# A conformer block on one core: a new written-out order of the instruction blocks, with new PSUM banks

## The chip, the cores and the metric

The kernel runs on one core of a Trainium2 chip. Each of the core's engines takes its instructions from a queue of its own, in the order in which the program wrote them: TensorE (PE, with its weight loads shown apart as PEld), ScalarE (ACT), VectorE (DVE), GpSimd (POOL) and SyncE (SP, which here only issues DMAs). Engines meet through semaphores. TensorE writes its results to PSUM, which has eight banks; ScalarE and VectorE read them there and write to SBUF.

The metric is the device time of one execution in microseconds, as the median of several runs. Next to it stands one profiled execution, whose trace gives the start and duration of each instruction. Its span runs from the first to the last instruction.

## The reference, cut to what matters

The input x has 2 sequences of 4000 tokens with 144 features. All tensors are bf16.

```python
h = _silu(_layernorm(x) @ w_ff1a) @ w_ff1b;  x = x + 0.5 * h       # 144 -> 576 -> 144
q, k, v = split(_layernorm(x) @ w_qkv)                              # 4 heads of 36
p = softmax(q @ k.T * 36 ** -0.5);  x = x + (p @ v) @ w_o           # 4000 x 4000 a head
a, b = split(_layernorm(x) @ w_pw1);  h = a * sigmoid(b)
x = x + _silu(depthwise_conv5(h)) @ w_pw2
h = _silu(_layernorm(x) @ w_ff2a) @ w_ff2b;  x = x + 0.5 * h
return _layernorm(x)
```

The attention is the bulk: 2 sequences, 4 heads and 4000 x 4000 scores each, 128 million exponentials.

## The kernel before, in words

**Tiling.** The 8000 tokens are 16 chunks of 500, eight to a sequence. A step of the attention takes one chunk of queries against 64 keys, for all four heads. Its scores fill two PSUM banks (128 partitions x 1000 values, as four matmuls of 64 x 500, `scores` and `emit_S`, L1770 and L1783). ScalarE turns them into a PT tile (bf16, 128 x 1000) by one Exp instruction (`emit_exp`, L1797), or VectorE does it with integer arithmetic in five instructions on two PT tiles (`dve_tile`, L1811). TensorE then multiplies the PT tile with the values (`o_quads`, L1847; "PV" below, four matmuls PS<-PT,VA) and accumulates in banks 6 and 7. Banks 0 to 5 are shared by the scores and by all other work, so that at most three pairs of score banks are in flight, and fewer while other work holds some. There are 15 PT tiles.

**The other work** runs beside the attention in small pieces: layer norms (statistics ST on VectorE, the power RS and the normalised rows XN on GpSimd), transposes through DRAM (tensor `rows`: four writing DMAs rows<-XN or rows<-AN and two reading ones XT<-rows, issued by SyncE, `blocks`, L1032), the feed-forward layers (HT; tanh tiles TH on ScalarE), the q, k, v projections, the gated unit and convolution (U, SW), and the residuals (X). GpSimd copies the edge columns between neighbouring chunks (`halo`, L1490, and L1505). Before about 20 us and after about 840 us there is no full attention to hide this work: the first chunk has to be made, and the last chunks have to be finished and stored.

**What sets the order.** A planner in the kernel's code writes all instructions down, in small blocks, with costs of its own. What the engines get is then decided by two tables written out by hand, ORDER (L38) and PLACES (L111). `Rec.reorder` (L281) sorts the blocks of each engine by ORDER: the table has one letter for each block of an engine, and the letter's place in ALPHABET (L37), less 45, says how many places the block moves from where the planner had it (P is no move, Q one later, O one earlier; ~ begins a wider move).

```python
            shift.append(c - 45)
...
        for i, blk in enumerate(blocks):
            at[i + shift[i]] = blk
        lines[e] = [o for blk in at for o in blk]
```

PLACES has a digit for each of 1724 PSUM tiles: the first bank that the tile takes. `reorder` then works out anew which reader of a bank has to be done before the next tile may be written there, and `finish` (L365) turns all dependences into semaphore waits. Nearly all instructions are recorded through one helper, so that the profile shows them under the same line, L419, and they are told apart by their tiles.

Of the kernel before, what the change touches and what calls it, by code (L numbers as in the profile page):

```python
# [39 lines left out]
        "PPPPPPPPQOPPPPROQNPPQRPQLPPRPVPSPNIZMWOMVVL~OVKLJ~OOJJNSNLMMMNPNPKSOOJ[JZKMXNKOG]NJHEKNNNE_MMMadMJLL"  # L40
        "mTLI?LJLEMZPbJNJMGrLLLLkfJKKKKKWKNNVJMKgBJJJ[QddGGMIFKEcQKLJFKNKKNNKPUMOMWTMYVIRLLISKOLPQQRPRPJQUNPQ"
        "OQKPPPPPYOOOOYNNNOMhTNLVXLMIMOSXKILOKN`NNRRNHQOXROMQOTKOUQQQTQUS]PT[`P2ALQXDMKILMNTQLSKNRNUN_PMMNOWN"
        "]NNOOSKPRPDIOQOY__MWNNN]NHMNQCGMQJNWNORTOMRRTLTPNSOBOP^UNNQMMTLNPTLLTMNOWNOOOXNOPLOPNQQMTTNNNNRSO]OQ"
        "OPPGPNROMQQLPPQOPVOcNNNNPMTNNOM]]LNNKMNPWOPNJUOOCOOXOOYZOMKcLLWXJKKSWKHKKVJNNKNORPNPQOQOSOOVNOYZMMMM"
        "NNOMPXPKOOVQMNPVOPHPYMNOQNNPN[]^LMM]MKWKKKLJKLVLP`LN_NLNOMOQNKMRMNLPPPQOS[P[MOPISOKNQMIPRPSPLQNPWORO"
        "QQKLVOQRN[QQQQJFPPPPKQQSPRKQQLPPPQVPPQOPUUOOPNCXORRNYVSSNG[MPUZPPAOKAOMUNNPVOLTUOL]KLNRPMMSNNNNdZNQM"
        "MMNNQMSLLTYMOMSHVKUO]JJ`RKTNQKMFLNQNW[]NLPHLNQNRMNFPPPS]OOLOOPPSLNNNQOSOPN`SNOMNO_PMMNOMOOLPNPYVL^[Q"
        "LNKKFMQM[TLMOOQWNQVQMKYNRNXNO8NRMMNYOOQNN^OOOQOIOSP[OPRPZGOOPN]YMNNNO<VNNKMNOYPNOOOTQM]MVJSMMRMKSPUM"
        "HOPNSOOOSOPNTPNOOROOQVNOPNO^RPQMVOHNQNLPRPJPXOOPNPNOOPXXNNNOOOWNIOOOORUOPKOSNROTXKOW[KOKLN[RZIMOIKNN"
# [12 lines left out]
        "OTKOPSSUHNSOOSHO^PUOOQNNGO_NNSMM[TMKSLMKYMJOMbQNLRLMXMNSMMMMYTMQWHMJPSLLQMVOROOLQUZXOMIMWPKMKMOQNQO`"
        "OPR`LMVLNLNPNJhPSHN]RHQMI^NQIMKTNVIOLHSXIQZIOVJMbMKZSPKQSIYKDLRKLMMSNTfNORUMRGLSULNWZLF_KP^KHYJPLLEM"
        "M]LL]cNUMVPKRLJLGPWPN;NNNZNOUNNZOLLSPMQIRSKPL]^_MMMMMMOMKMMMSSLRNKPPWOVNOOLNNQRNOVTNNWXLLLQMSLSKMOQO"
        "TPNRZ_MKNNNWQLZ^LJHLQKKXLWMKMMPTQVK[QOLUPMZPMMQVMPVVLMYLOMQUN`NNNP[QN%SLMMMOWQMI[QMSMKNNVSMOLLTNQNNP"
        "WQV[LPNJKPSKOOLPQOQO_QNNXNNVMMMOMKMP_OOOOOQNQOPKWOOPKQN`YOOROOPFOQNROEQQUYJVNNPJOOJ[OOPNPROLYTNKMNTM"
        "NNNP^[NOMNNQMMOLNN]PNOOR[OPKQN_ZLNESMOOKHOM[NPPLPNOOPPMQSTMNPQQQQRSQRRTCQVNGRNOMTTTMMNUPPQHNQSPMYVTQ"
        "KLLSSOIJPSSPTMKORNOQOPPPPPPSORNSMRNRRRNQQRPFRPQQQQQQRPFQO"
    ),
    "act": (  # L70
        "PPPPPPPPPPPPPRTNNOOPPQOPPPPPPXPNOSNNNNPPPPPPQRSOLOQZQORKRSLLOQQJPPPPQQNQOPPPPPPPPPQQQMPPPPPPPPPPPPRO"
        "OPQOPQQNPPPPPPPPPPPPPPPPPPPPPPPPPPPPPPPPPPPPPPPPPPPPPPPPPPPPPPPPPPPPPQOPRORNSNOOPPPPPPPPPQOPPPPPPPPP"
        "QOPPPPPPPPPPPQOPPPPPPPPPPPPQOPPPPPPPPPPPRPNPQOPPPPPRPNPPPPPPPPPPPPPPPPPPPPPPPPPPPPPPPPPPPPPPPPPPQOQQ"
        "NPPPPPPPPPPPPPPPPPPPPPPPPPPPPPPPPPPPPPPPPPPPPPPPPPPPPPPPPPPPPPPPPPPPPQOPPPPPPPPPPPPPPQOPPQOPPPPPPPPP"
        "PQOPPPPPPPPPPPPPPPPPPPPPPPPPPPROOPQOPPPPPPPPPPPPPPPPPPPQOPPPPQOPPPPPPPPPPPPPPPPPTOOPQQLPPPPPPPPPPPPP"
        "PPPPPQOPPQOPPPPPPPQOPPPPPPPPPPQOPPQOPPPPPQQQQLQQNPPPPPPQOPPPPPPPPPPPPPPPQOPPPQOPPPPPPPPPPPPPPPPPPPPQ"
        "OPPPPPPPTOPNOROOPPPPPPPPPPPPPPPQOPQOPPPPPPPPPPQOPPPPPPPPPPPQOPPPPPPPPPPPPPPPPQOPPPPPPPPPPQOPPPPPPPPP"
        "PPPRPNPPPPPPPPPQOPPPPPPPPPPPPPPPPPPPPPQRNOPPQQNPPPPPPPQQNPPPPPPPPPPPPPPPPPQOQOPPQOPPPPPPPPPPQOQOPPPP"
        "PPPQOQOPPPPPPPPPPPPPPPPPPPPPPPPPPPPQQNPPPPPPPPPPPPPPPPPPPPQOPPPPPPPPPPPPPPROOPPPPPPPPPPPPPPPPPPPPPQQ"
        "NPPPPQOPPPPPPPQQNPPPPPPPPPQOPPPPPPPPPPPPQOPPPPPPPPPPPPPPPPPPPPPPPPPPPPPPPPPPPPPPPPPPPPPPQOPPPPPPPPPP"  # L80
        "PPPPPPPPPPPPPPPPPPPPPPPPPPPPPPPPPQOSPNRNOQOUQNPMOPPPRORNQNPPPPPPQOROQQMPPPPPPQOPPPWORNNNOO"
    ),
# [23 lines left out]
    "sp": (  # L106
        "PPQOPPPPQOPPPPPPPPPPPPPPPPROOPPPPSOSNNOPPPPPPPPPPPPPPPPPQOPPQOPPQOPPQOQOPPPPPPQOPPPPPTOPNRNOVOOOOOOP"
        "WOVNNNNOMPPSORNQMPPPPSOOOPPWOQNNOOOPPPPQSNOOPPQQN"
    ),
}  # L110
PLACES = (  # L111
    "2354210532250435102310543130213550204405323252304105230054110122532115431241204124012410314032034023"
    "4203420340243310402430043213420342040324303025420342034203420342034203420342034203420342024042045012"
    "4024120552405240424052405240425025203540240532052402405240524052402205304230532052305240524052405245"
# [2032 lines left out]
```

## Time and profile before

| | |
|---|---|
| median of 3 runs | 879.83 us (879.45 to 880.12) |
| the profiled execution's own time | 878.56 us |
| its span | 876.7 us |
| granted TensorE clock, mean | 0.998 |
| TensorE, ScalarE, VectorE, GpSimd busy | 96%, 97%, 94%, 34% of the span |
| DMA | 28.82 MB, 33 GB/s |

The busy time of an engine counts each moment once. ScalarE's records of neighbouring instructions overlap, since the next one starts before the last one's end is recorded; the pace is therefore read as busy time of a group divided by its count, not from the mean duration of one record. An idle stretch is put down to the instruction that ended it.

### The profile page before, as it was taken

Reading aid. Unit: us, or ns where it says so; the run is one execution under the profiler, and the core shown is the slowest. Engines: PE = TensorE matmul, PEld = TensorE weight load, DVE = VectorE, ACT = ScalarE, POOL = GpSimd, SP = SyncE. Lnnn points to the kernel's source line nnn. Section 1 sums busy time; section 2 is a strip of 40 time slices with the busy share of each in tenths; the row PEclk is TensorE's granted clock in tenths of the full one; section 3 lists DMA queues with packets and bytes.
Section 4 is the critical chain, followed back from the end, with each engine's and each line's share of the span. In section 5 each row is a group of like instructions: output and inputs, shape, how many; then the busy total and the mean of one; then the engine's idle time right before and its main releaser. Section 6 shows DMA issues by size and latency. Waiting matters only on the chain.

```text
span 876.7 us, 27043 instructions
## 1 busy us (share of the span) xinstructions
PE 844.4 (96%) x11419; PEld 385.5 (44%) x11419; DVE 825.6 (94%) x1821; ACT 848.4 (97%) x1098; POOL 293.8 (34%) x573
## 2 busy tenths in 40 slices
PE   8999999999999999999999999999999999999996
PEld 6544444334444434443444444444434443344465
DVE  8978999999999999999989999899999999999987
ACT  6799999999999999999999999999999999999985
POOL 6650441341425231152324426222420115013434
PEclk9999999999999999999999999999999999999999
DMA  3221101211121020212001120100210010001111
GB/s 100 52 52 35 26 15 41 58 29 38 37 48 41 16 52 9 45 22 53 16 4 35 28 46 16 36 24 16 49 26 22 16 31 19 21 14 37 29 25 35
DMA packets 114353, 28.82 MB, mean 33 GB/s; under 512 B 101090, under 2 KB 114230, under 8 KB 114230
## 3 DMA queue, kind: packets, MB, share of 16 engines
q1 hardware_dynamic: 112646, 26.39, 13.7%
q8 instruction: 90, 1.47, 0.7%
q10 hardware_dynamic: 1584, 0.69, 0.3%
q14 instruction: 33, 0.27, 0.1%
HBM read 13.44 MB, written 13.61 MB: 31 GB/s over the span
## 4 chain that ended last, share of the span: by engine, by line
PE 39%; ACT 35%; DVE 21%; POOL 3%; issue 1%; DMA 0%; POOLq 0%; DVEq 0%
PE PS L419 39%; ACT PT L419 32%; DVE PT L419 10%; ACT TH L419 3%; DVE ST L419 3%; DVE HT L419 2%; DVE X L419 2%; DVE XN L419 2%; POOL RS L419 1%; POOL XN L419 1%; DVE QT L419 1%; DVE AN L419 0%; DVE KT L419 0%; DMA X<-in_x_dram 0%; DVE VA L419 0%
## 5 line engine op out<-in xcount | busy, mean ns | idle before, releaser
L419 ACT ACTIVATE PT<-PS 128x1000 bf16<-128x1000 f32 (+1 forms) x818 | 751.0, 1048 | 3.7 <-PE PS L419 2.6
L419 PE MATMUL PS<-QT,KT 64*64 64x500 bf16 x3968 | 419.2, 383 | 15.6 <-ACT PT L419 8.5
L419 PE MATMUL PS<-PT,VA 64*37 64x500 bf16 x4728 | 403.1, 372 | 1.0 <-DVE QT L419 0.7
L419 DVE TENSOR_SCALAR PT<-PS 128x500 int16<-128x500 f32 x380 | 251.2, 669 | 6.2 <-PE PS L419 4.7
L419 PEld LDWEIGHTS PS<-QT,KT 64*64 64x64 bf16 x3968 | 125.1, 104 | 231.8 <-ACT PT L419 122.4
L419 POOL TENSOR_SCALAR RS<-ST 125x4 f32<-125x4 f32 x130 | 39.5, 304 | 484.0 <-DVE ST L419 477.7
L419 PEld LDWEIGHTS PS<-PT,VA 64*37 64x37 bf16 x4728 | 141.9, 96 | 91.4 <-issue 13.1
L419 DVE TENSOR_SCALAR PT<-PT 128x1000 uint16<-128x1000 uint16 x380 | 153.1, 418 | 2.1 <-PE PS L419 0.9
L419 POOL TENSOR_SCALAR XN<-X,RS 125x144 bf16<-125x144 bf16 x260 | 146.8, 594 | 8.3
L419 DVE TENSOR_TENSOR PT<-PT 128x1000 bf16<-128x1000 bf16 x190 | 127.9, 675 | 1.1
L419 ACT ACTIVATE TH<-PS 128x500 bf16<-128x500 f32 (+3 forms) x194 | 101.1, 542 | 5.4 <-PE PS L419 4.4
L419 POOL TENSOR_TENSOR RS<-RS,NHALF 125x4 f32<-125x4 f32 (+1 forms) x93 | 92.0, 993 | 33.8 <-DVE RS L419 28.3
L419 DVE SCALAR_TENSOR_TENSOR HT<-TH,PS 128x500 bf16<-128x500 bf16 (+1 forms) x135 | 80.9, 615 | 8.6 <-ACT TH L419 7.9
L419 PE MATMUL PS<-XT,WA 80*128 80x500 bf16 (+5 forms) x288 | 74.4, 364 | 3.5 <-DVE XT L419 1.1
L419 DVE BATCH_NORM_STATS2 ST<-X 125x6 f32<-125x288 bf16 x160 | 65.6, 448 | 1.0 <-DMA X<-in_x_dram 0.9
L419 DVE SCALAR_TENSOR_TENSOR X<-PS,X 125x288 bf16<-125x288 f32 (+1 forms) x128 | 57.1, 451 | 6.8 <-PE PS L419 5.5
L419 PE MATMUL PS<-WB,HT 128*125 128x144 bf16 (+1 forms) x640 | 52.4, 230 | 0.8 <-ACT HT L419 0.5
L419 PEld LDWEIGHTS PS<-WB,HT 128*125 128x125 bf16 (+1 forms) x640 | 44.2, 136 | 14.6 <-issue 4.0
L419 PEld LDWEIGHTS PS<-XT,WA 128*128 128x128 bf16 (+1 forms) x288 | 21.2, 97 | 37.9 <-issue 9.8
L419 DVE STREAM_TRANSPOSE XN<-XN 128x320 f32<-128x320 f32 x54 | 27.2, 503 | 3.3 <-POOL XN L419 2.5
L419 PE MATMUL PS<-U,DG 128*128 128x250 bf16 (+6 forms) x204 | 29.3, 264 | 0.5 <-DVE PT L419 0.2
L419 POOL COPY U<-U 128x2 bf16<-128x2 bf16 (+1 forms) x54 | 10.0, 222 | 50.9 <-DVE U L419 50.9
(95 smaller groups left out, 520.1 us busy)
## 6 DMA issues: line engine op xcount, KB each, us to landing
rows<-XN SPq DMA_DIRECT2D x216, 40.0 KB, 2.0
XT<-rows SPq DMA_DIRECT2D x56, 128.0 KB, 2.0
rows<-AN SPq DMA_DIRECT2D x60, 40.0 KB, 2.0
X<-in_x_dram SPq DMA_DIRECT2D x15, 140.6 KB
XTQ<-rows SPq DMA_DIRECT2D x26, 70.3 KB
out_dram<-XN SPq DMA_DIRECT2D x13, 140.6 KB
XT<-rows SPq DMA_DIRECT2D x56, 16.0 KB, 1.8
out_dram<-XN SPq DMA_DIRECT2D x3, 70.3 KB
```

Source lines behind the costliest of these rows:

```text
L419: ins = getattr(eng, o.name)(*o.a, **o.k)
```

## The change

Only the two tables are replaced. The planner, the instructions, their sizes and their number stay; which exponentials go to VectorE stays too. In numbers, from the letters of both tables:

| engine | blocks | blocks at another place | widest move |
|---|---|---|---|
| TensorE | 2855 | 1981 | 24 |
| ScalarE | 1093 | 97 (43 of them in its last tenth) | 8 |
| VectorE | 1689 | 904 | 21 |
| GpSimd | 125 | 92 | 10 |
| SyncE | 157 | 64 | 8 |

Of TensorE's blocks, 926 of the 1069 PV blocks move, 461 to an earlier place and 465 to a later one, by 4 places on average; 496 of the 851 blocks that hold scores alone move, by at most 5 places; 236 of the 347 blocks that hold scores of a VectorE tile with PV matmuls between them move. Of the 1724 PSUM tiles 154 get other banks, 58 of them among the last 124 tiles and 15 among the first 100.

The diff, cut to the first line of some tables (the rest is of the same kind):

```diff
 ORDER = {
     "pe": (
-        "PPPPPPPPQOPPPPROQNPPQRPQLPPRPVPSPNIZMWOMVVL~OVKLJ~OOJJNSNLMMMNPNPKSOOJ[JZKMXNKOG]NJHEKNNNE_MMMadMJLL"
+        "PPPPPPPPQOPPPPROQNPPQRPQLPPRPTPUPNIZOVOKVVL~OOKOK~OUHINSNLMMMOPNOJSOOL[I[KMYMKOGRNJHFKOOOE^NNN_dMKLM"
...
     "act": (
-        "PPPPPPPPPPPPPRTNNOOPPQOPPPPPPXPNOSNNNNPPPPPPQRSOLOQZQORKRSLLOQQJPPPPQQNQOPPPPPPPPPQQQMPPPPPPPPPPPPRO"
+        "PPPPPPPPPPPPPRTNNOOPPQOPPPPPPXPNOSNNNNPPPPQOPPSPNOQZQORKRSLLOQQJPPPPQQNQOPPPPPPPPPQQQMPPQOPPPPPPPPRO"
...
     "pool": (
-        "PPPPPPPQOPPPPPPQOPQQQQQQJPQOPPP_OOOOOSNNNSWLTNLJNNPPQOSOOTNPNOTUNNNNQNPPSOPNPPPQSUMOPPQJPPQTRMNNQOPQ"
-        "OVOOPNOQNPPPRPQM"
+        "PPPPPPPROOPPPSOPNPQQQQQQJPPPPPP_PPPPPJOOPQ[NKTMMOMNOSNUMNSNRNTKVNVMPLMPMROQTMOOTVMNNNOQTMOOQXMOOOTNN"
+        "OMPPQOPPUOQNNOPPQOPQQNROO"
...
 PLACES = (
-    "2354210532250435102310543130213550204405323252304105230054110122532115431241204124012410314032034023"
+    "3054320451505435202310543130213550204405323242301405230054110122532155431241204124012410314032034023"
...
```

Two moves that the prediction looks at. On GpSimd the copy of chunk 0's right edge into chunk 1's left one (U<-U) goes from place 40 to place 31 of the queue, from behind nine layer-norm blocks to before them. On SyncE the four writes rows<-AN of the second finished attention chunk (AN1) go from place 36 to place 29, and four writes rows<-XN (XN1) from place 24 to place 31, so that XN2's writes, place 31 before and 30 now, stand between them.

More of the change, by code (lines that the diff above doesn't have):

```diff
@@ L45 @@
[L45 to L49, printed above, removed]
@@ new lines @@
+        "nXMJ@LJMFMYGaJNKMJhLLLLljKKKKKKWKMMWNKK`BJJJQRecHFSIGKH]QKMRGKPMJJMMQTNPNXTRSUJUJJJSLPMPPQUQQNKOTOOR"
+        "OQLPPPPPYOOPN[NNNOMfRNLYULMIMOS^KIMOJNaNNQMNHPPaUOMQNYKPSPPQUSVV^QQ^_Q5<@QCPMKIMNNTQMSMNSNUOYQKMMOQQ"
+        "^MSOORNOPPCOORPZP^O]OOO[OCNOQEHMUJNNTOMR[MQWXMPMMNNDMPXSNNZMMTMMMTMPLMPP]OOOOQQNUKNOMQMP]WNOMPNVKYPN"
+        "JNQHNOOPQQQMPPQOPUP]MNNNOOTNNOMNWOPPMPNOW]VNN[MMHMKYMMQ]YKI`JLQYJJKV[KHMJTLJOJPMQORPVMQNYMN]MN[bLLLL"
+        "LMNLPRPKWOYFMNOVNOHXXMKOLNNNN[[_MMMTLLTKKKLJOOPRP`MO_OMNOMPQLLMRMMMPPPQOSYP[MOOISOLNPPIPSPTOLRNNWPNO"
@@ new lines @@
+        "QQMMPUQRN[QQQRJFPPPPJQQSPPKQQNPPPPVPPQOPVXOOPNDNPRROSVSYNFWMPYUPNDPJFPNPTOPYOLOPNQ[NLNRPMRLNNOPhUNZM"
+        "MMNLNNPMMWYLPNZKNLMF[LPPSLVINLNOMWQNYPYPLQHKOSNORPGPPPS[OOLOOPPYLNNNVOMNOM^QMNTOO_KMMNOMPPLPNQOYL]RY"
+        "LMKLMMPLY]KLNNQXMRXSLI[MDObNOENPMMNSNNQMMWNNNOSVNiKZNNQOTFNNOMXXUMMMM?TLLIYMQXXLLMMQZMJJ`ORLMUMKQYNL"
+        "INPMMUVNLNOMYPMOORNNRUNKPNO_ROQLSSKMQMKPROLPSOORNOSOOOTVNNNNSNTMTMNNOVXNOMORLSNVXIMSYLMKLN^XYNLMNHMM"
+        "WLLMXMNYMOLNNXMNXMMVMM[SLJLLZN^OLNNJUbLLLQNLPRGNNOOOPNRNOPPPeOOOOPSOOORROf`OPNO^@QDLJLMOLTKLTMTRKGMQ"
@@ new lines @@
+        "QNUOPNROYYPZOHNbILLLLbTLLSLLLLPLM_M[MMMMMcMMMMNLMOdZMNNNNIMMMMXMNNVOMKMMZNOUaMMMQMM]^HOMKNNNJZMKM[LM"
+        "QgLLLMWMMMMU]LLLV^MQJMWTMHBHMZSKL[PLLZTMK_bMMIGbMPLPQMSVCKRKSMBINPPSPVOLOOOOZQNNS[MMMMNSMOMNO]aNNcMM"
+        "MMMMMMNLNNNZWNZMZPNKPMYBENOPJYNNPMPQOLQNPPRRO[YQJNOPQOPXFPHPNOOOPWOOOOOOXPMTQOLOK^OXNNOMPPPLPPHQQNgR"
+        "cOLQOMPNOOOOdRM@LdOJOIPIOOOJOOOOJOOPNUPNOOQQYLQ]NLZ[LLLdWKIKLLLWULE]LLLLLOMWRcKLLLNZM[PMMRILNKZJ`[JK"
+        "MOLLUbKeJLLYKOUKMMMMMY=KMNNZNL^NLNNNNNN_NNNOQQNPTHNN_NLOOO^QMNPKO^QQM_JFPLOPJMNPPLPhMPROOPQOWOWNNNNU"
@@ new lines @@
+        "=KQAQRNQQEPPPPPPPQOQOSOSOhTPMPRMSEOOKOPPPPPPROGNOPPPQRNRNOPQQQMPPPPPQQNQQNQQQQQKQQQRVOXOHOOLOOQNRPNP"
+        "PPPPPPPSOOWNSNNQMUQKSOOQJQUN^PhLNKOPPKOKNNNPPMOOOOOOOOQQQRRKNPRPRPSQOQTPTODNRNQNQQUPLPROTRPWMXSNPSQW"
+        "RZQUFOSDO7KOPPPTOOSOTOPPIPPPQOPPPPPPTPQMQMPQOPQQNQQRRORRRUQRPUWTQNRSCTRPRRRRDQQRPSPRSQR[RTQNPREO~NKO"
+        "RNaNOOOPQMNQYNOPNPTQFNJPRRNNPPPPQOPQOPUPPPPSQOVVFNNNNNPPROOPPPPPROQNPPQQNPPRORPUPTQINLPPQOQOPPPPQOQQ"
+        "RMTPPROUQRPFLQRNOPPROOUOXNNNUMNVWL[PRVIGPIOINQNPQQRTUSOITJPKOPSQS`PQQRHRSSTVSWWGRGW<FHMWWMVLLMTMKLO"
@@ L109 @@
+        "VOWNNNNPMOPVOZNOMNNOOSNNNPPZOPNOOOOOOOPXOOOOOPPQLPPPPPPQO"
     ),
@@ L130 @@
+    "0412041201412042041204024012412140214021401240214042303250540316224455153562430123441101203205424135"
+    "154252140154303532026214"
 )
```

110 lines of the change are left out of this document (46 added, 64 removed).

## The prediction

> **What bounds the kernel now.** I read the page first, then busy times by stage, then the groups of ScalarE's and TensorE's instructions in the middle stage, then the chain of work at the end.
>
> The page's busy times, and its chain by engine:
>
> ```profile
> span 876.7 us, 27043 instructions
> PE 844.4 (96%) x11419; PEld 385.5 (44%) x11419; DVE 825.6 (94%) x1821; ACT 848.4 (97%) x1098; POOL 293.8 (34%) x573
> PE 39%; ACT 35%; DVE 21%; POOL 3%; issue 1%; DMA 0%; POOLq 0%; DVEq 0%
> ```
>
> Three engines are nearly full, and the chain changes between them all the time. Busy time by stage (start, PE, PEld, DVE, ACT, POOL):
>
> ```profile
> 0.00:60.00 60.00, 54.69 (x612) 33.30 (x613) 51.38 (x151) 47.26 (x82) 41.93 (x94) 1.00 0.30 70
> 60.00:840.00 780.00, 759.86 (x10474) 327.94 (x10472) 744.40 (x1567) 776.00 (x956) 238.52 (x454) 1.00 0.14 30
> 840.00:876.70 36.70, 29.80 (x338) 24.27 (x336) 29.87 (x105) 25.10 (x63) 13.32 (x26) 0.95 0.11 30
> ```
>
> From 60 to 840 us ScalarE is idle for 780.0 - 776.0 = 4.0 us only, against 20.1 for TensorE and 35.6 for VectorE. By this ScalarE bounds the middle and an order of blocks has 4 us to win there. But its records overlap, so a late start hides in a busy second. The pace shows it: the exponentials of a full tile in the whole middle, and one undisturbed series of 27 of them (start, time, count):
>
> ```profile
> L419 ACT ACTIVATE PT<-PS 128x1000 bf16<-128x1000 f32 x782 | 724.3, 1057 | 2.6 <-PE PS L419 1.7
> 777.56 24.00 ACT L419 ACTIVATE PT<-PS 128x1000 bf16<-128x1000 f32 x27
> ```
>
> On average a tile takes 724.3 / 782 = 926 ns of ScalarE, in the series 24.00 / 27 = 889 ns. The difference, 37 ns on 782 tiles, is 29 us: the most that better feeding could give in the middle. Does it vary from place to place? The same group in six stretches of 130 us; here the best paced, 450 to 580, and the worst, 320 to 450:
>
> ```profile
> L419 ACT ACTIVATE PT<-PS 128x1000 bf16<-128x1000 f32 x128 | 118.4, 1047 | 1.0 <-PE PS L419 0.9
> L419 ACT ACTIVATE PT<-PS 128x1000 bf16<-128x1000 f32 x130 | 120.9, 1060 | 0.1
> ```
>
> 925.0 and 930.0 ns; the other four lie between. Six stretches with different work and different orders agree within 5 ns, so 2.5 ns either way, which on 782 tiles is 2 us. That is the first hint of the size: another order of the same sort moves the middle by some 2 us, not by 20.
>
> **The change part by part.** Nothing is added or removed, so each term is a wait that moves.
>
> *Middle, TensorE.* ScalarE starts late when the scores come late, and the scores come late when TensorE stands at something else. What ended the idle time before its weight loads, 60 to 840 us:
>
> ```profile
> L419 PEld LDWEIGHTS PS<-PT,VA 64*37 64x37 bf16 x4664 | 140.3, 96 | 89.4 <-issue 11.9 <-DVE PT L419 9.7 <-DVE QT L419 2.7
> L419 PEld LDWEIGHTS PS<-QT,KT 64*64 64x64 bf16 x3880 | 122.7, 104 | 226.8 <-ACT PT L419 120.4 <-DVE PT L419 28.2 <-issue 19.5
> ```
>
> Scores wait 120.4 us for ScalarE to free a bank: that is the bound showing itself, and no order takes it away. The PV blocks wait 9.7 us for a PT tile of VectorE: these are blocks that stand in the queue before their data, with ready work behind them, and this is what an order can mend. 926 of 1069 PV blocks are moved, so this term is decided anew. It can go to nothing (-9.7 us on TensorE) or double (+9.7). I take a third of it as a gain that reaches ScalarE, **-3.2 us**: a third, because up to three score pairs stand between the two engines and a short wait is absorbed, and because the six stretches allow some 2 us. That it is a gain rather than a loss is a choice; I checked it on two of the widest moves, the first on GpSimd. The copy U<-U goes before nine layer norms. Its present time, the blocks between which it will stand, and the writes of its data:
>
> ```profile
> 178.73 2.64 POOL L419 TENSOR_SCALAR XN<-X,RS 125x144 bf16<-125x144 bf16 x4
> 190.97 0.28 POOL L419 TENSOR_SCALAR RS<-ST 125x4 f32<-125x4 f32 x1 [9.61 <-DVE ST L419]
> 279.54 0.31 POOL L419 COPY U<-U 128x2 bf16<-128x2 bf16 x2
> L419 DVE SCALAR_TENSOR_TENSOR U<-TH,PS x2: 286/462/639, 183.8 to 185.1; 64x125 bf16<-64x125 bf16 x1, 128x500 bf16<-128x500 bf16 x1
> ```
>
> It moves from 279.5 into the gap from 181.4 to 191.0, and its data are there by 185.1 + 0.6 = 185.7. GpSimd sat idle there for 9.6 us, which hides the copy's 0.3, and nothing is held up. If U came 5.3 us later, the layer norm behind it would be late.
>
> *Middle, DMA queue.* The second wide move puts AN1's four writes on SyncE before those of XN2, and XN1's right behind. The transposes that make the data (AN, XN), SyncE's issues and TensorE's first use:
>
> ```profile
> 168.51 0.50 DVE L419 STREAM_TRANSPOSE AN<-AN 128x320 f32<-128x320 f32 x1
> 170.09 0.50 DVE L419 STREAM_TRANSPOSE XN<-XN 128x320 f32<-128x320 f32 x1
> 157.43 2.55 SPq L419 DMA_DIRECT2D rows<-XN  x4
> 170.62 3.64 SPq L419 DMA_DIRECT2D rows<-XN  x4
> 175.71 0.83 SPq L419 DMA_DIRECT2D XT<-rows  x2
> 200.19 3.35 SPq L419 DMA_DIRECT2D rows<-AN  x4
> 180.81 0.61 PE L419 MATMUL PS<-XT,WP 128*128 128x500 bf16 x2
> XT<-rows SPq DMA_DIRECT2D x56, 128.0 KB, 2.0
> ```
>
> AN1 is ready at 169.0 and holds the queue for 3.35 us, to 172.4; XN2's writes start there instead of at 170.6 and end at 176.0; XN1's four take 2.55 more; the reading DMAs go out at 178.6 instead of 175.7, and with the median 2.0 us land at about 181. TensorE wanted them at 180.8. So the cover of 2.9 us is used up and not exceeded: nothing lost, but what comes late next is TensorE's gated-unit block, by as much as any of these is later than here. The other moves on SyncE (the stores, up to 8 places later) have nobody waiting at once. **0**, with 1 us of loss as the other end.
>
> *Middle, the rest.* ScalarE's own order changes in about twenty small groups of neighbours, mostly a tanh tile swapped with an exponential, whose work covers it. VectorE's moves are mostly by one place; it has 35.6 us of idle time in the middle. New banks change which reader a score waits for; that is inside the 120.4 us. All **0** for themselves, and within the ends above.
>
> *The end, from 840 us.* The chain of work there is VectorE without a break for 18 us, first and last pieces and the last ones of all:
>
> ```profile
> 848.17 0.46 DVE X L419
> ...
> 866.26 0.18 DVE RS L419
> 866.51 1.02 POOL RS L419
> 867.55 1.00 DVE XN L419 x4
> 868.55 0.38 DVE X L419
> ...
> 872.34 0.32 DVE XN L419
> ```
>
> ```profile
> 867.30 0.84 PE L419 MATMUL PS<-WB,HT 128*125 128x144 bf16 x10
> ```
>
> The work on VectorE is the same after the change, so this part can shrink only by what the last chunk's path no longer waits for. The XN piece at 867.55 belongs to chunk 11, which is not the last; in the new table it stands three places further up. The residual X behind it, of the last chunk, starts at 868.55, and TensorE's product for it (second fence) is done at 867.30 + 0.84 = 868.14: of the 1.00 us of the piece only 0.4 can be had. **-0.4**, with the ends -1.0 (the whole piece) and +1.0: ScalarE's table brings HT tiles up to 8 places forward here, and one that isn't ready holds the row behind it.
>
> *The start.* 8 of ScalarE's first 109 blocks move by one or two places and TensorE's by 1.2 on average. ScalarE is idle for 12.7 us up to 60 us, which covers a swap. **0**, 1 us either way.
>
> Sum: -3.2 + 0 - 0.4 + 0 = -3.6 us. The profiled execution took 878.56 us, 1.9 more than its span, and becomes 875.0, its span 873.1. The median of the three runs is 879.83, 1.27 above that execution; with the same difference the forecast is **876.2 us**. Its own range goes from 879.8 - 9.7 - 1.0 = 869.1 up to 878, where no difference begins.
>
> [...]
>
> [...]
>
> **The rivals.**
>
> *No difference (879.4; within 0.2% is 878.1 to 881.6).* For it: the even pace. Against: the series at 889, which shares its instructions with all others.
>
> *Slower: TensorE's head of the queue.* 461 PV blocks move to an earlier place. If half as many again stand before their PT tile as now, the 9.7 us grow by 4.9, and with ScalarE full all of it comes through: 879.8 + 4.9 = **884.7**. It decides where a wait outlasts the one tile that ScalarE has in hand, 0.89 us; shorter ones are absorbed. For it: the even pace shows that the present order is at least good everywhere, and VectorE, whose tiles are waited for, is the engine with the longest idle time, so the least regular. Against: the two places checked fit the trace. [...]
>
> *Much faster.* Half of the 29 us goes: 865. It needs the 37 ns to be waiting that the new order ends everywhere.
>
> *It isn't what it says*: if the intervals are not the chip's, the new places are as good as chance, and that is the no-difference case widened by the 2 us of the stretches.
>
> **How the numbers follow.** Something like 0.2%, 1.8 us, is what a measurement of this kernel can tell from no change. The forecast has 0.40, much faster 0.05, no difference 0.22, slower 0.33 (the head of TensorE's queue 0.25; the same on ScalarE or SyncE at the end or around 176 us 0.08). Faster is then 0.45, same 0.22, slower 0.33. The range reaches from the forecast's lower end to the slower case with the losses of the DMA queue and the end on it, 884.7 + 1.0 + 1.0: **869.0 to 886.7**. It leaves out much faster below and, above, a doubling of the 9.7 us, some 0.1.
>
> **What would show it.** Right: in the middle, full tiles at 920 to 924 ns of ScalarE (now 926), with PV's wait for VectorE's PT below 9.7 us; the copy U<-U at about 186 us; the read into XT near 178.6; the last part from 840 shorter by 0.4 us. Wrong: the same pace (no difference), or PV's wait at 14 us and more and TensorE's idle time above 20 (slower). If the time changes and the middle does not, the end or the start did it, and my term for the middle is wrong.

## The result, and the profile after

| | before | after |
|---|---|---|
| median | 879.82 us (879.45 to 880.12) | 875.36 us (875.23 to 875.51) |
| the profiled execution's own time | 878.56 us | 875.47 us |
| its span | 876.7 us | 873.7 us |

The ratio after to before is 0.995, with a 95% interval from 0.9932 to 0.9967. The forecast was 876.2 us. The profiled execution of before lies 1.3 us under its median, so the two traces differ by 3.0 us and the medians by 4.5; what follows goes by the traces.

The page of after, with the lines that answer to those shown of before:

```profile
span 873.7 us, 27060 instructions
PE 844.9 (97%) x11419; PEld 385.8 (44%) x11419; DVE 825.3 (94%) x1821; ACT 845.2 (97%) x1098; POOL 294.8 (34%) x573
ACT 65%; PE 20%; DVE 11%; POOL 3%; issue 1%; POOLq 0%; ACTq 0%
```

ScalarE's share of the chain of waits went from 35 to 65%. TensorE and VectorE had 39 and 21% and have 20 and 11: they hold ScalarE up less.

The groups of after from 60 to 840 us, ScalarE's full tiles and TensorE's weight loads for PV and for the scores:

```profile
L419 ACT ACTIVATE PT<-PS 128x1000 bf16<-128x1000 f32 x782 | 724.8, 1059 | 2.6 <-PE PS L419 2.0
...
L419 PEld LDWEIGHTS PS<-PT,VA 64*37 64x37 bf16 x4672 | 141.1, 96 | 93.2 <-issue 12.7 <-DVE PT L419 8.1 <-ACT PT L419 6.3
L419 PEld LDWEIGHTS PS<-QT,KT 64*64 64x64 bf16 x3880 | 122.2, 104 | 225.0 <-ACT PT L419 128.4 <-DVE PT L419 24.0 <-issue 16.4
```

A full tile takes 724.8 / 782 = 927 ns, as before (926). The prediction wanted 920 to 924 here. By this marker nothing happened in the middle; yet the middle is where the time was won. That is seen when one asks when ScalarE is done. ScalarE's table load stands behind the last exponential; here it is before, and after:

```profile
841.60 1.28 ACT L419 ACT_TABLE_LOAD   x1
```

```profile
837.79 1.28 ACT L419 ACT_TABLE_LOAD   x1
```

It comes 3.81 us sooner. The first exponential starts 0.34 us sooner (18.75 against 19.09 us; in the profiles of this study it lies between 18.6 and 23.5, so this bit is scatter), so the middle is 3.5 us shorter. The rest, by the busy times of that last stretch (start, end, length, PE, PEld, DVE, ACT, POOL), before and after:

```profile
841.60:876.70 35.10, 28.20 (x332) 23.59 (x329) 29.40 (x105) 23.52 (x59) 11.83 (x16) 0.95 0.12 31
```

```profile
837.80:873.70 35.90, 29.11 (x330) 24.20 (x326) 30.27 (x105) 23.41 (x59) 12.43 (x23) 0.94 0.12 31
```

The end became longer by 0.8 us, and VectorE is busy for 0.87 us more in it, with the same 105 instructions. So: start -0.3, middle -3.5, end +0.8, together -3.0.

Where in the middle? TensorE's own idle time, ahead of the matmuls and not of the weight loads, before and after:

```profile
L419 PE MATMUL PS<-QT,KT 64*64 64x500 bf16 x3883 | 411.1, 383 | 15.2 <-ACT PT L419 8.5 <-DVE PT L419 2.8 <-DVE VA L419 0.3
L419 PE MATMUL PS<-PT,VA 64*37 64x500 bf16 x4664 | 397.7, 372 | 1.0 <-DVE QT L419 0.7 <-DVE PT L419 0.2
```

```profile
L419 PE MATMUL PS<-QT,KT 64*64 64x500 bf16 x3880 | 410.8, 383 | 11.7 <-ACT PT L419 7.4 <-DVE PT L419 0.9 <-DVE SW L419 0.4
L419 PE MATMUL PS<-PT,VA 64*37 64x500 bf16 x4672 | 401.4, 372 | 1.8 <-DVE QT L419 1.0 <-DVE PT L419 0.5 <-ACT PT L419 0.2
```

Before the scores it fell by 3.5 us, before PV it rose by 0.8. It is the scores that come sooner, not the PV blocks. (That 3.5 is also the middle's gain is partly chance: all of TensorE's idle time from 60 us to the table load fell from 20.1 to 17.5 us.) When each exponential of one trace is set beside the same one of the other, the gain is a sum of many small steps, some of them losses; the largest that the next exponentials don't give back is 0.87 us, at 551 us of before. There VectorE, TensorE and ScalarE of before stood one after the other:

```profile
550.46 0.51 DVE L419 STREAM_TRANSPOSE XN<-XN 128x320 f32<-128x320 f32 x1 [0.40 <-POOL XN L419]
550.89 0.64 DVE L419 TENSOR_SCALAR PT<-PS 128x500 int16<-128x500 f32 x1
```

```profile
551.68 0.41 PE L419 MATMUL PS<-QT,KT 64*64 64x500 bf16 x4 [0.62 <-ACT PT L419]
```

```profile
552.13 1.00 ACT L419 ACTIVATE PT<-PS 128x1000 bf16<-128x1000 f32 x1 [0.42 <-PE PS L419]
```

VectorE waits 0.40 us for GpSimd's normalised rows and only then reads the scores in bank 0, until 551.53. By the table PLACES the next scores go to banks 0 and 1, and they start at 551.68. The profile puts TensorE's 0.62 us down to ScalarE, but the read that ended last before 551.68 is VectorE's. In the new order the transpose stands two places further back, and none of the three waits is there.

### The profile page after: what moved, and what is told of

Its sections match the earlier page's. It is cut to its first block, busy times and chain, and to the rows that moved or that the text cites. A ratio compares the mean times of both kernels' runs of the same rounds, so it can differ in the third digit from the quotient of the medians.

```text
span 873.7 us, 27060 instructions
## 1 busy us (share of the span) xinstructions
PE 844.9 (97%) x11419; PEld 385.8 (44%) x11419; DVE 825.3 (94%) x1821; ACT 845.2 (97%) x1098; POOL 294.8 (34%) x573
## 4 chain that ended last, share of the span: by engine, by line
ACT 65%; PE 20%; DVE 11%; POOL 3%; issue 1%; POOLq 0%; ACTq 0%
ACT PT L419 60%; PE PS L419 20%; ACT TH L419 5%; DVE PT L419 4%; DVE ST L419 2%; DVE XN L419 2%; POOL XN L419 1%; DVE X L419 1%; POOL RS L419 1%; DVE HT L419 1%; DVE RS L419 0%; DVE AN L419 0%; DVE U L419 0%; DVE KT L419 0%; DVE XT L419 0%
## 5 line engine op out<-in xcount | busy, mean ns | idle before, releaser
L419 POOL TENSOR_SCALAR XN<-X,RS 125x144 bf16<-125x144 bf16 x260 | 144.9, 587 | 9.6 <-DMA out_dram<-XN 1.5
L419 POOL TENSOR_TENSOR RS<-RS,NHALF 125x4 f32<-125x4 f32 (+2 forms) x93 | 93.9, 1013 | 33.6 <-DVE RS L419 28.1
L419 PE MATMUL PS<-XT,WA 128*128 128x500 bf16 (+4 forms) x288 | 75.6, 368 | 3.4 <-DVE PT L419 0.8
L419 DVE SCALAR_TENSOR_TENSOR X<-PS,X 125x288 bf16<-125x288 f32 x128 | 56.7, 450 | 4.9 <-PE PS L419 3.6
L419 POOL COPY U<-U 128x2 bf16<-128x2 bf16 (+1 forms) x54 | 12.2, 266 | 56.2 <-DVE U L419 56.2
```

The source lines that it names most:

```text
L419: ins = getattr(eng, o.name)(*o.a, **o.k)
```

## The experiments

The theory at the outset was the prediction's (PV blocks nearer to their data). The rivals: another part of the change made the gain, or the parts work only together. Ratios are to the kernel before, measured on the same chip along with the run, with their 95% intervals.

### TensorE's PV blocks alone

The PV blocks from 60 to 836 us stand where the new table has them; all else is as before. This kernel and the next four were put together in stretches of 20 us, and no block passes a cut between two of them.

```diff
     "pe": (
...
-        "mTLI?LJLEMZPbJNJMGrLLLLkfJKKKKKWKNNVJMKgBJJJ[QddGGMIFKEcQKLJFKNKKNNKPUMOMWTMYVIRLLISKOLPQQRPRPJQUNPQ"
+        "nTLI?LJLEMZPaJNJMGhLLLLljJKKKKKWKMMWNKK`BJJJQRecGGSIGKH]QKMRGKPKLJNLQTNPNXTRSUJUJKISLPMPQQUQQNJOTOPR"
...
```

> The kernel before, in which only TensorE's PV blocks stand where the new table has them, from 60 to 836 us of the trace of before; scores, other work, banks and the four other engines stay as before. In the traces the last exponential starts at 839.96 us before and 836.24 after. Theory (the prediction's term for the middle: PV blocks nearer to their data): most of these 3.7 us are had by this alone, the last exponential starts at 836.5 to 837.5, PV's wait for VectorE's PT tiles falls from 9.7 to about 8 us, and the time is 876.5 to 877.5. Rival (the gain comes from another part: banks, VectorE's order or ScalarE's): last exponential at 839.5 to 840.5, time 879.3 to 880.3.

Measured: 902.75 us, ratio 1.0265 (1.0251 to 1.0279). Neither case: 23 us slower. The groups from 60 to 840 us, weight loads and matmuls of PV, VectorE's reads of scores, and ScalarE's tiles:

```profile
L419 PEld LDWEIGHTS PS<-PT,VA 64*37 64x37 bf16 x4502 | 131.5, 96 | 105.4 <-DVE PT L419 21.5 <-issue 15.8 <-ACT PT L419 3.4
...
L419 PE MATMUL PS<-PT,VA 64*37 64x500 bf16 x4498 | 389.0, 373 | 9.0 <-DVE PT L419 7.6 <-DVE QT L419 1.0
...
L419 DVE TENSOR_SCALAR PT<-PS 128x500 int16<-128x500 f32 x370 | 244.4, 668 | 14.8 <-PE PS L419 12.8
...
L419 ACT ACTIVATE PT<-PS 128x1000 bf16<-128x1000 f32 x760 | 707.0, 1030 | 14.0 <-PE PS L419 11.4
```

These rows fit a ring. PV waits for VectorE's tiles (loads 9.7 before, 21.5 now; TensorE's own idle time 1.0 before, 9.0 now); the scores behind them come late, so VectorE, which needs scores too, waits (PE's part 4.7 before, 12.8 now), its tiles come later still, and ScalarE waits along (1.7 before, 11.4 now).

### TensorE's whole table and the banks; VectorE's order alone

With TensorE's table and the banks:

```diff
     "pe": (
...
-        "mTLI?LJLEMZPbJNJMGrLLLLkfJKKKKKWKNNVJMKgBJJJ[QddGGMIFKEcQKLJFKNKKNNKPUMOMWTMYVIRLLISKOLPQQRPRPJQUNPQ"
+        "nTLI?LJLEMZPaJNJMGhLLLLljJKKKKKWKMMWNKK`BJJJQRecHFSIGKH]QKMRGKPMJJMMQTNPNXTRSUJUJJJSLPMPPQUQQNKOTOOR"
...
 PLACES = (
...
-    "4203420340243310402430043213420342040324303025420342034203420342034203420342034203420342024042045012"
+    "4203421340243310402430043213420342040324304023420342034203420342034203420342034203420342024042045012"
...
```

and with VectorE's table:

```diff
     "dve": (
...
-        "PROUXM~P:~P2~P<~P2KLJLLLDLNKPMILMMGSLJKLJKMJOLJTOILJHLJOQNPIFHMNNKMMMMBMXPIKINIPLLLNOCNCOQOKQQDFWUVE"
+        "PROUXM~P7~P2~P3~P6KLJLLLDLNKPMILMMGSLJKLJKMJOLJTOILJHLJOQNPIFHMNNKMMMMBMXPIKINIPLLLNOCNCOQOKQQDFWUVE"
...
```

> The kernel before with TensorE's whole new order and the new banks from 60 to 836 us (in 37 of 39 stretches of 20 us; in the other two the order stays as before), the four other engines as before. Theory: as with the PV blocks alone, 876.5 to 877.5, since scores and banks add nothing. Rival 1, banks or scores decide: 876 here, and 879.8 with the PV blocks alone. Rival 2, the order of VectorE or ScalarE decides: 879.8 here too. Rival 3, the tables of the engines are tuned to each other and one alone does harm: above 881.

> The kernel before with VectorE's new order from 60 to 836 us (in 36 of 39 stretches of 20 us, 646 of its 904 moved blocks), all else as before. Theory (PV blocks decide): within 0.5 us of before, 879.3 to 880.3. Rival, VectorE's tiles come earlier by its own order and that shortens TensorE's wait: 877 to 878 with the last exponential at 837 to 838 us.

Measured: 908.59 us, ratio 1.0333 (1.0318 to 1.0349), and 908.74 us, ratio 1.033 (1.0316 to 1.0345). The third rival of the first text is what came, for both kernels: one engine's table alone does harm. That this is so because the tables are tuned to each other is borne out by the pair below. (How much of the loss is the cuts' is told there too.)

### TensorE and VectorE together; all orders with the old banks

Both engines' tables and the banks are those of the two kernels above, now in one (first); then all five orders, shown at ScalarE's, and no new bank:

```diff
     "dve": (
...
-        "PROUXM~P:~P2~P<~P2KLJLLLDLNKPMILMMGSLJKLJKMJOLJTOILJHLJOQNPIFHMNNKMMMMBMXPIKINIPLLLNOCNCOQOKQQDFWUVE"
+        "PROUXM~P7~P2~P3~P6KLJLLLDLNKPMILMMGSLJKLJKMJOLJTOILJHLJOQNPIFHMNNKMMMMBMXPIKINIPLLLNOCNCOQOKQQDFWUVE"
...
```

```diff
     "act": (
...
-        "PPPPPPPPPPPPPRTNNOOPPQOPPPPPPXPNOSNNNNPPPPPPQRSOLOQZQORKRSLLOQQJPPPPQQNQOPPPPPPPPPQQQMPPPPPPPPPPPPRO"
+        "PPPPPPPPPPPPPRTNNOOPPQOPPPPPPXPNOSNNNNPPPPPPQRSOLOQZQORKRSLLOQQJPPPPQQNQOPPPPPPPPPQQQMPPQOPPPPPPPPRO"
...
```

> The kernel before with the new order of TensorE and VectorE and the new banks, from 60 to 836 us (37 of 39 stretches of 20 us); ScalarE, GpSimd and SyncE and both ends as before. With TensorE's PV blocks, its whole table or VectorE's table alone the time rose by 23 to 29 us: the two fit only each other. Theory: they are the pair that makes the middle, the moves of ScalarE, GpSimd and SyncE do little, and the last exponential starts at 836 to 837.5 us, the time is 2 to 3.5 us under before. Rival: ScalarE's 41 moved blocks of this stretch belong to it as well, and without them the time is above before by 2 us or more.

> The kernel before with all five engines' new orders from 60 to 836 us (38 of 39 stretches), but the PSUM banks of before, where 77 tiles of these stretches would get others. Theory (the order makes the gain, the banks are for nothing): last exponential at 836 to 837, 2.5 to 3.5 us under before. Rival (the banks decide for which reader the next scores wait, and are fitted to the order): 77 tiles with up to 0.9 us each to lose, so last exponential at 840 or later, and the time at or above before.

Measured: 888.68 us, ratio 1.0101 (1.0088 to 1.0115), and 894.2 us, ratio 1.0163 (1.0149 to 1.0177). Taken at their word, both rivals hold. But the cuts have a share in it. When each exponential is set beside the same one of before, the time that is lost (or won, -) between 4 and 18 us behind a cut, and from 2 us ahead of a cut to 4 us behind it, is in all:

| kernel | away from the cuts | around them |
|---|---|---|
| after (has no cuts) | -4.6 us | +1.4 us |
| PV blocks alone | +13.8 | +8.3 |
| TensorE's table and banks | +16.3 | +11.1 |
| VectorE's order alone | +15.9 | +8.5 |
| TensorE and VectorE | 0.0 | +8.6 |
| all orders, old banks | +3.8 | +9.8 |

The table puts what is lost between two exponentials to the later one. Put to the earlier one, up to 2.4 us change columns (away from the cuts, after then has -2.2, the pair +1.2, the old banks +6.0), so a difference of 2 us in it says nothing.

For one engine alone the loss outlasts the cuts: 14 to 16 us lie away from them. For TensorE and VectorE together it does not: nearly all of it lies around my cuts, and elsewhere the pair stands within about 1 us of before. The first text's rival is not borne out, nor is its theory: without the moves of ScalarE (41 blocks there), GpSimd and SyncE the pair does hardly any harm, and has no net gain. Which of these three engines it lacks was not tried. The old banks cost 3.8 + 4.6 = 8.4 us away from the cuts (8.2 by the other way of counting), and most of it in three stretches (140 to 160 us, 700 to 720, 780 to 800). TensorE's idle time before the scores with them, from 60 to 840 us:

```profile
L419 PE MATMUL PS<-QT,KT 64*64 64x500 bf16 x3820 | 406.7, 385 | 16.1 <-ACT PT L419 6.6 <-DVE PT L419 3.7 <-DVE X L419 0.8
```

It is up from 11.7 to 16.1 (cuts included). The middle's 3.5 us can't be shared out among the engines in this way: no engine's part has a net gain of its own.

### The end

The first kernel has all tables of after up to 836 us of before's trace and those of before from there; here ScalarE's last line, after against this kernel:

```diff
     "act": (
...
-        "PPPPPPPPPPPPPPPPPPPPPPPPPPPPPQOPPRORPMSPPULOSNRMMPPPPQTPSOKSQOKROORPQQLPPPPPPRORRRWRJRRMHMROO"
+        "PPPPPPPPPPPPPPPPPPPPPPPPPPPPPPPPPQOSPNRNOQOUQNPMOPPPRORNQNPPPPPPQOROQQMPPPPPPQOPPPWORNNNOO"
...
```

> The kernel after up to 836 us of the trace of before, on all engines; from there the order and the banks of before. From the last exponential to the end of the span it is 36.7 us before and 37.4 after, so the traces say that the end became longer by 0.7 us where the prediction had it shorter by 0.4. Theory (the end's own order is worse): 874.7, faster than after by 0.7 us. Rival (the end is longer since VectorE reaches it with more work left, 30.3 us busy behind the last exponential instead of 29.4, whatever the order there): as after, 875.2 to 875.7. Prediction's term (new order at the end is better by 0.4): 875.8.

Measured: 876.34 us, ratio 0.9965 (0.9951 to 0.9978). Undecided: the end is short again (36.8 us behind the last exponential), but the cut itself cost 1.6 us at 833 to 836 us of the trace, where the exponentials fall from 0.4 us ahead of after's to 1.2 us behind them. Hence two cuts at a cleaner place, where each engine but GpSimd has done the same blocks by both tables: after and then before (ScalarE's last line is that of the diff above), and the reverse, before and then after:

```diff
     "act": (
...
-        "PPPPPPPPPPPPPPPPPPPPPPPPPPPPPPPPPQOSPNRNOQOUQNPMOPPPRORNQNPPPPPPQOROQQMPPPPPPQOPPPWORNNNOO"
+        "PPPPPPPPPPPPPPPPPPPPPPPPPPPPPQOPPRORPMSPPULOSNRMMPPPPQTPSOKSQOKROORPQQLPPPPPPRORRRWRJRRMHMROO"
...
```

> The kernel after up to about 797 us, the kernel before behind it, cut on every engine but GpSimd where both tables have done the same blocks. By the traces nearly all of the middle's gain is had by then (3.5 of 3.7 us). From the last exponential to the end it was 36.7 us before, 37.4 after, and 36.8 with the order of before from 836 us on. Theory (this length belongs to the order that is used there): 36.7 us again, and the time 0.5 us under after. Rival (VectorE comes to the end with more work, whatever the order): 37.4, the time as after.

> The reverse: before up to about 797 us, after behind it. Theory: the last exponential starts as before, at 839.8 to 840.2, the end takes 37.4 us, and the time is 0.5 us above before. Rival: the end takes 36.7 and the time is that of before. By the prediction's term for the end (0.4 us shorter) it would be 0.4 us under before.

Measured: 875.4 us, ratio 0.9948 (0.9935 to 0.996), as after; and 879.98 us, ratio 1.0004 (0.9995 to 1.0013), as before. So the whole gain that a clock can see is made before 797 us. The times can't decide 0.5 us; the traces can. From the table load to the end, with the end of before, and with the end of after:

```profile
838.60:873.70 35.10, 28.21 (x332) 23.59 (x329) 29.41 (x105) 23.55 (x59) 11.85 (x16) 0.96 0.12 31
```

```profile
841.70:878.00 36.30, 29.11 (x330) 24.20 (x326) 30.34 (x105) 23.49 (x59) 12.50 (x23) 0.97 0.12 30
```

VectorE's busy time goes with the order of the end, whatever came before: 29.4 us in these kernels with the old one, 30.3 with the new one. The length goes with it less strictly: over the other kernels of this study with a granted clock of 0.994 to 0.999 that have the old end it lies between 34.8 and 35.8 us, against 35.9 and 36.3 with the new one. The theory holds as far as that shows. The 0.9 us are not more work. By kind and count VectorE has the same 105 instructions there in either order; in the new one it begins them later. The first ones, before and after:

```profile
841.13 0.68 DVE L419 SCALAR_TENSOR_TENSOR HT<-TH,PS 128x500 bf16<-128x500 bf16 x1 [1.90 <-ACT TH L419]
```

```profile
837.88 0.51 DVE L419 STREAM_TRANSPOSE XN<-XN 128x320 f32<-128x320 f32 x1 [1.67 <-POOL XN L419]
```

The first starts 0.5 us ahead of the table load in before, behind a wait for ScalarE, and 0.1 us behind the load in after, behind a wait for GpSimd. The rest of the 0.9 us is that the others follow one another less closely.

### PV without its wait for VectorE

```diff
...
+            if o.acc is not None and o.name == "matmul" and any(d.eng == "dve" and d.kind == "e" for d, raw in o.deps if raw):
+                o.deps = [(d, raw) for d, raw in o.deps if not (raw and d.eng == "dve" and d.kind == "e")]
+                o.k["rhs"] = o.const
...
+            if o.eng == "dve" and o.kind == "e":
+                o.deps = [(d, None if raw is False and d.eng == "dve" and d.kind == "e" and d in made else raw)
+                          for d, raw in o.deps]
...
-               acc=(ph, p, k), **flags)
+               acc=(ph, p, k), **flags).const = WA1[64 * p:64 * p + 64, 0, 0:CH]
```

> The kernel before, its tables untouched, but the PV matmuls of VectorE's tiles read a weight tile that is long there instead of the PT tile, and so never wait for VectorE (VectorE still makes its tiles; the attention's result is wrong by that part). It prices the wait that the prediction's middle term is made of: 9.7 us of the PV weight loads for VectorE's PT. By the prediction at least a third of it reaches ScalarE: 3.2 us under before, up to 9.7. New theory: the loads run ahead of the matmuls and wait while TensorE still works; TensorE itself stood idle only 1.0 us before PV matmuls in the middle, so 0 to 1.0 us under before, last exponential at 839 to 840 us.

Measured: 882.53 us, ratio 1.0037 (1.0026 to 1.0048): slower, which neither case had. TensorE's matmuls from 60 to 840 us (WA,VA are the PV matmuls that no longer wait), and VectorE's work on its tiles:

```profile
L428 PE MATMUL PS<-QT,KT 64*64 64x500 bf16 x3872 | 410.2, 383 | 16.2 <-ACT PT L428 8.8 <-DVE PT L428 2.4 <-DVE VA L428 0.3
L428 PE MATMUL PS<-PT,VA 64*37 64x500 bf16 x3132 | 301.2, 372 | 0.2 <-DVE QT L428 0.2
L428 PE MATMUL PS<-WA,VA 64*37 64x500 bf16 x1508 | 156.8, 372 | 0.5 <-DVE QT L428 0.5
```

```profile
L428 DVE TENSOR_SCALAR PT<-PT 128x1000 uint16<-128x1000 uint16 x377 | 153.2, 421 | 3.5 <-PE PS L428 0.9
```

TensorE's idle time before PV fell from 1.0 to 0.7 us, no more: the 9.7 us belonged to loads that ran ahead of working matmuls. The kernel has one change too many, though: since PV no longer orders two uses of a PT slot, VectorE has to wait for its own earlier write there (the three lines of the diff on VectorE), and its idle time before PT<-PT rose from 2.1 to 3.5 us. That may be part of the 3 us; the rest stays open. So the time of this run prices nothing, and the idle time does: TensorE had 1.0 us to win there, not 3.2.

### Five transposes one place back

```diff
     "dve": (
...
-        "PVPNOOUOPLOTPSPNQIROOPSPPMPQOPPPPPPQQQMQOPRROQQKPPPPPPPPPPQOPSOSNSOROJTOOOORPNSOPTTPKMNPPPPPPPPPPQXP"
+        "PVPNOOUOPLOTPSPNQIROOPSPPMPQOPPPPPPQQQMQOPRROQQKPPPPPPPPPPQOPSOSNSOROJTOOOORPNSOOTTPLMNPPPPPPPPPPQXP"
...
```

> The kernel before, in which five blocks of VectorE's order change: the five transposes XN<-XN that wait for GpSimd in the middle (1.9 us together, at 354, 550, 616, 706 and 734 us) each go one place back, behind a block that is ready. At 551 us, where the traces of before and after drift apart most in one step (0.87 us), VectorE stood 0.40 us before such a transpose, and read the scores in bank 0 that much later; TensorE's next scores waited for that bank, and ScalarE stood 0.42 us. Theory (waits of VectorE for others hold PSUM banks, and this is where the new order gains, not at the PV blocks): 0.4 to 0.9 us are won at 551 us, up to 1.5 with the other four, and the last exponential starts at 838.5 to 839.5. Rival (PV's places or the banks made the step): within 0.3 us of before at each place.

Measured: 878.46 us, ratio 0.9987 (0.9979 to 0.9996), table load at 840.84 instead of 841.60 us. Five blocks moved by one place bring it forward by a fifth of what the whole change does (0.76 of 3.81 us). The place at 551 us now:

```profile
550.51 0.68 DVE L419 TENSOR_SCALAR PT<-PS 128x500 int16<-128x500 f32 x1
551.10 0.50 DVE L419 STREAM_TRANSPOSE XN<-XN 128x320 f32<-128x320 f32 x1
```

```profile
551.34 0.41 PE L419 MATMUL PS<-QT,KT 64*64 64x500 bf16 x4
```

The three waits are gone, and this place alone wins 0.55 us. The other four win 0.18 (616 us), 0.15 (734) and nothing (354, 706). A step of 0.38 us the other way, at 272 us, where nothing was moved, warns that the two small ones could be chance; the step at 551 us stands clear of it. What fits is the block that now goes first: at 551, 616 and 734 us VectorE reads scores (PT<-PS) and so frees a bank for the next ones; at 354 it works on HT, whose source is in PSUM too but is no scores, and at 706 on a tile in SBUF.

### TensorE without most of PV

```diff
+        gone = {id(o) for o in lines["pe"]
+                if o.acc is not None and o.acc not in (first[o.acc[:2]], final[o.acc[:2]])}
+        lines["pe"] = [o for o in lines["pe"] if id(o) not in gone]
...
```

> The kernel before without the PV matmuls that are neither the first nor the last of their accumulation (the attention's result lacks them), which takes some 390 us of work from TensorE, all waits of ScalarE and VectorE as before. It asks what ScalarE can do when TensorE is never late. Prediction's rival (the 926 ns of a full tile are ScalarE's own): the last exponential starts at 839 to 840 us as before. Against it (a late TensorE costs ScalarE some 24 to 29 us in the middle): 811 to 818 us, starts of neighbouring full tiles 884 to 890 ns apart throughout. Third: VectorE, 744 us busy in the middle, takes over as the bound before that, and the gain is 10 us or less.

Measured: 951.78 us, ratio 1.082 (1.0801 to 1.084). None of the three: 72 us slower with 6781 matmuls instead of 11419, some 390 us of work less. The page's busy times, and its slices of TensorE's busy time and granted clock, in tenths:

```profile
PE 821.4 (86%) x6781; PEld 324.3 (34%) x6781; DVE 837.7 (88%) x1821; ACT 863.8 (91%) x1098; POOL 288.6 (30%) x573
PE   8999987888888889898977988798888889898897
PEclk9996689577998786968799898969878865758779
```

With less to do TensorE was granted less clock in this run, 0.80 on average against 0.998. From 60 to 840 us a score matmul lasts 470 ns on average (383 before). ScalarE's busy time goes with the clock, as two stretches of 20 us show (start, end, length, PE, PEld, DVE, ACT, POOL, clock, DMA):

```profile
100.00:120.00 20.00, 19.15 (x160) 5.71 (x162) 16.27 (x32) 16.81 (x18) 6.72 (x14) 0.52 0.15 32
480.00:500.00 20.00, 15.88 (x154) 6.93 (x154) 16.39 (x34) 20.00 (x28) 5.48 (x13) 1.00 0.01 2
```

Of the ten stretches of 40 us from 60 to 460 us, the three at a clock of 0.88 to 0.96 have ScalarE busy for 38.6 to 39.2 us, the seven at 0.63 to 0.80 for 33.2 to 36.9. That the clock is a good part of the loss is the author's estimate from these rows; how much of the 72 us it makes was not taken apart. The order was made for a TensorE that has PV to do, and this kernel too makes VectorE wait for its own earlier writes of PT. As a test of ScalarE's floor the run is void.

### After with nine more moves, and the end of before

Nine blocks of VectorE change places with a block that is ready while VectorE waits, and from 838 us on all tables are those of before.

```diff
     "dve": (
...
-        "PQRPQRRORPQFPPPPPPPPPWPNPNOOOUPNOPNQSNSNNSNORNUQMPMOPROOROVNOOOPQMPPPPPPXQNQMQUNQNSOUQQUCOJOOPPQQNQO"
+        "PQRPQRRORPQFPPPPPPPPPWPNPNOOOUPNOPNQSNSNNSNORNUQMPMOPROOROVNOOOPQMPPPPPPXQNQMQUNQNSOUQQUCOJOOPPPQOQO"
...
```

> The kernel after with two changes. First, nine blocks of VectorE's order, found in the trace of after: where VectorE stands 0.3 to 1.1 us before a block (5.4 us together) and one of the next two is ready by the trace, that one goes first; the waits can shrink by 4.1 us. Second, the order of before from 838 us on, cut on each engine but GpSimd where both tables have done the same blocks. Theory: five such moves in the kernel before shortened VectorE's waits by 1.6 us and brought the last exponential forward by 0.76 us, so these nine bring 1.5 to 2 us, the last exponential at 834.2 to 834.8 instead of 836.24; the end takes 36.7 us instead of 37.4; together 2 to 2.7 us under after, ratio to before 0.992 to 0.993. Rival (after has no wait of VectorE left that reaches ScalarE): last exponential at 836.0 to 836.5, only the end gains, ratio 0.994.

Measured: 874.76 us, ratio 0.9945 (0.9932 to 0.9959). It beats before, and can't be told from after (0.995). The last exponential starts at 836.53 us, later than in after (836.24) and than either case had it; the first one starts 0.66 us later here, by scatter, and the seam costs some. Of the nine moves one wins, 0.69 us at 561 us. It too is a transpose that waits for GpSimd, and behind it stands a read of scores; in after, and in this kernel:

```profile
561.37 0.51 DVE L419 STREAM_TRANSPOSE XN<-XN 128x320 f32<-128x320 f32 x1 [0.96 <-POOL XN L419]
561.81 0.64 DVE L419 TENSOR_SCALAR PT<-PS 128x500 int16<-128x500 f32 x1
```

```profile
560.90 0.68 DVE L419 TENSOR_SCALAR PT<-PS 128x500 int16<-128x500 f32 x1
561.76 0.51 DVE L419 STREAM_TRANSPOSE XN<-XN 128x320 f32<-128x320 f32 x1 [0.18 <-POOL XN L419]
```

At this place after had lost what the move wins: against before its exponentials fall back there by 0.7 us. The other eight, whose forward blocks read no scores, win nothing that the trace shows, though VectorE waits less there. The estimate that half of the waits' shortening reaches ScalarE was wrong; here it is all or nothing. The new seam at 838 us costs 0.5 us, and the end behind it is 35.0 us long, as with before's order.

## Why the forecast came out right, and which of its steps did not

**The total.** Forecast -3.6 us for the profiled execution; the spans differ by 3.0. The sum stands on two terms, one with about the right size and a wrong cause, one with the wrong sign. That the total came so close is partly luck.

**The bound.** ScalarE bounds the middle: that held. The yardstick did not. "The pace is therefore read as busy time of a group divided by its count", it said, but that still counts a late start as work, because the records overlap (one lasts 1057 ns on average, and neighbours start 884 ns apart, so a start up to some 0.17 us late leaves no gap); it read 926 and 927 ns for two middles that differ by 3.5 us. The six stretches that agreed within 5 ns therefore said nothing about what an order can win. The start of the last exponential is the better measure.

**The middle, -3.2.** Measured -3.5. The step that failed is "the PV blocks wait 9.7 us for a PT tile of VectorE ... and this is what an order can mend". After the change the sign that was asked for is there, since the loads' wait for VectorE's tiles fell from 9.7 to 8.1 us; but they now wait 6.3 us for ScalarE's tiles (no more than 2.7 before), so PV waits longer for PT tiles in all. TensorE's own idle time before PV was only 1.0 us to begin with and rose to 1.8, and without the wait for VectorE (if with a new one in its place) the kernel was not faster. The line "scores wait 120.4 us for ScalarE to free a bank ... no order takes it away" was right to be set aside: it rose to 128.4. The wait of the scores for VectorE stands in the same row, and the prediction gave it no term: 28.2 us of their loads before, 24.0 after, and of TensorE's own idle time before them 2.8 and 0.9. Of the 3.5 us by which that idle time fell, 1.9 are VectorE's and 1.1 ScalarE's. VectorE's moves and the new banks, which decide when it frees those banks, were set at 0 for themselves. One cause of the gain is shown, VectorE's wait ahead of a read of scores: five moves of VectorE alone win 0.9 us, 0.55 of it at one place. The 0.69 us of the ninefold change are no part of the 3.5, since after had lost them. That the third of 9.7 came close was luck. What makes the other steps, most of them 0.1 to 0.5 us, was not taken apart; most of the middle's gain has no shown cause.

**The two moves that were traced.** Right, both. The copy U<-U stands at 185.12 us (expected about 186), its wait covered. The DMAs around 176 us, in the trace of after:

```profile
168.14 2.59 SPq L419 DMA_DIRECT2D rows<-AN  x4
170.78 6.33 SPq L419 DMA_DIRECT2D rows<-XN  x8
177.15 1.08 SPq L419 DMA_DIRECT2D XT<-rows  x2
```

The eight writes of XN2 and XN1 follow AN1's four, and the reads go out at 177.15 us (expected 178.6; AN1's writes started 0.9 us sooner than expected and took 2.59 us, not 3.35). TensorE takes the data at 180.1, no later than before (180.8): 0, as said.

**The end, -0.4.** Measured +0.8. The step that failed is "the work on VectorE is the same after the change, so this part can shrink only": the work is the same, even behind the last exponential, but when VectorE begins it and how closely it follows is a matter of the order, and its busy time there grew from 29.4 to 30.3 us.

**The rivals.** "No difference" (879.8 less the end's 0.4) falls with the interval. It needs the 926 ns of a full tile to be ScalarE's own time, with no waiting in them, which no run shows: neighbouring full tiles start 884 ns apart in the median of either trace, and the middle did gain. "Slower by the head of TensorE's queue" did not happen here, but the run with the PV blocks alone resembles it, and costs more than the rival's price: with PV's wait at 21.5 us, 11.8 more than before, the time was up by 23 us, 13.8 of them away from the cuts. That VectorE feeds back into it fits the rows of that run and was not tested by itself.

## What to carry to other kernels

Where several in-order engines feed each other, treat their orders and the banks as one object: in this kernel one engine's part of a good re-ordering lost 23 to 29 us, 14 to 16 of them away from the cuts, where the whole won 4.5. Who cuts such an order to test a part of it should cut where both versions have done the same blocks, and count what the cut itself costs. Of the fourteen single moves tried here the four that won time (two of them under 0.2 us) brought forward a block that frees what the bounding engine's next input needs, and the ten others won nothing; look for that block, not for the longest wait. And judge the bounding engine by when its last instruction starts, since busy time per instruction hid late starts here: with records of 1057 ns that start 884 ns apart it read 926 and 927 ns for two middles that differ by 3.5 us.

## What the runs showed of the hardware

With 6781 matmuls instead of 11419 TensorE was granted less clock: from 60 to 840 us the mean was 0.79, with TensorE busy for 674 of 780 us, against 1.00 at 760 of 780 before. After, the kernel with the PV blocks alone, the first one with the end of before and that with PV without its wait for VectorE had 1.00 there, with 746 to 762 us.

```profile
60.00:840.00 780.00, 673.68 (x5416) 243.45 (x5412) 691.29 (x1431) 723.21 (x875) 210.40 (x407) 0.79 0.13 27
```

What lowers the clock was not shown, nor where between 674 and 746 us busy it begins to fall. In this one experiment less work for TensorE came with a lower clock and a longer time, 951.78 us.
